# First half of the first batch's x turned by DMA inside the fold, and VectorE sums tied behind the addition for c12

## The chip, the cores and the metric

The kernel runs on one core of a Trainium2 chip. The engines that matter here are TensorE (PE: matmuls and transposes, with its weight loads as PEld), VectorE (DVE), ScalarE (ACT), GpSimd (POOL) and SyncE (SP), whose queue issues most of the DMAs. Each engine works through its own instructions in order. The metric is the device time of one execution in microseconds (us); lower is better.

## The reference

q, k and v are fp32; the weights come in as 8-byte floats, which the kernel converts to fp32 itself. Eight batches (B) of eight heads (H) have 576 tokens (S) of 64 values (D):

```python
kv = np.einsum('bhsd,bhse->bhde', k, v)
out = np.einsum('bhsd,bhde->bhse', q, kv)
rms = np.sqrt(np.mean(out * out, axis=-1, keepdims=True) + 1e-06)
attn = out / rms * g_norm
x = attn.transpose(0, 2, 1, 3).reshape(4608, 512)   # tokens x (heads, values)
out = (((x @ w1) * (x @ w2)) @ w3) @ w_out           # 512 -> 1024 -> 1024 -> 512
```

## The kernel before

**Groups.** The 4608 tokens are worked on as nine groups of 512: 512 of the 576 tokens of each batch make a group, and what is left over of all batches makes the last. For a group the kernel forms `kv` (L334), turns q so that tokens lie in the free dimension (on PE at L353, or by DMA), forms the attention product (L410), normalizes it (`norm`, L378 to L388, result in tile `xn`), and turns the normalized x into tile `xT`. Then the feed-forward part runs on `xT`: "gates" are the two products with `w1` and `w2` and their elementwise product (`gates`, L640 by `winograd`), in four passes p = 0 to 3 over the hidden columns, and "project" is the product with the folded matrix.

**The fold.** Since `w3` and `w_out` follow each other with nothing between, they are multiplied into one matrix `w3o` first (`fold_chunk`, L619, with the turned `w3` from `turn_w3`, L606, copied by ACT at L611). The fold has two halves of eight chunks c = 0 to 7. Its second half is interleaved by hand with the attention part of batch 0: at c = 1 and 4 come `kv` and q of two pairs of heads each (`begin_kv`, `begin_q`), at c = 2 and 5 the attention product of a half (`first.product`), at the start of c = 3 and 6 the end of its normalization, and at the end of c = 3 and 6 the turning of that half of x (`first.turn`, L444: eight 128x128 transposes on PE into two PSUM banks, which ACT copies to `xT` at L446). Weights are converted all along (`begin_next`: ACT at L158 and L159; `end_next`: DVE at L161 to L171, and a scaling by g at L136 on DVE or L134 on ACT).

**Turning by DMA.** `turn_by_dma` does the same without PE: a copy sorts the two 16-bit halves of each word apart (L291 or L293), SP issues a DMA transpose (L295), and a second copy puts the words together again (L305). `x_by_dma` does it for half of x, in two parts. Later batches use it with POOL's copies, batch 1's first half with ACT's.

**A pass of the gates.** `winograd` forms a 2x2 block product with seven products instead of eight. In order: a11·b11, s1·t1, s2·t2, s4·b22, s3·t3, a12·b21, a22·t4. Here a are the weights, s their sums (`sum_w(p)`, L692 and L693, four DVE operations into `ws` and `w_sb`), b are quarters of `xT`, and t their differences (`combine_x`, L682). Partial results are accumulated in three PSUM banks; ACT copies intermediate states out (L653), DVE adds (L778) and multiplies (L779). The tiles matter: u2 and u3 share one buffer `u`, so the copy of u3 has to wait until the addition for c12 has read u2, and the seventh product, which goes on in the bank that u3 is copied from, has to wait for the copy:

```python
        u2 = keep("u2", r1)
        between()
        product("s4", "b22", r2)
        done("c12", r2, u2)
        product("s3", "t3", r1)
        done("c22", p5, keep("u3", r1) if keep_u3 else r1)
        r3 = product("a12", "b21")
        done("c11", r3, p1)
        between()
        product("a22", "t4", r1)
        done("c21", r1, None)
```

**What sets the order.** PE, POOL and SP run in the order in which the program is written (`manual_schedule`). DVE and ACT are in written order inside the fold. In the groups after it a scheduler places their instructions; `tc.issue_after(x)` holds instructions back behind x. In group 0 (T = 0) the four passes also carry the conversions of the remaining weights, the sums of the next pass's weights (`sum_w(p + 1)`), and, for the product after the gates, the sums of `ab` and the differences of `w3o` (`sum_ab`, `combine_w3o`, L692, L693 and L682 on 256 columns). `between()` runs, twice in a pass, a piece of the next batch's attention part.

Of the kernel before, what the change touches and what calls it, by code (L numbers as in the profile page):

```python
# [22 lines left out]
def kernel(  # L23
# [32 lines left out]
    nc = tc.nc  # L56
# [7 lines left out]
    KF = DF // P  # L64
# [19 lines left out]
        return pool.tile([P, 512], FP32, name=tag, tag=tag)  # L84


    loaded, copies = {}, {}
    q_left = {}

    kv_left = [const.tile([P, H, D], FP32, name=f"{name}l_sb") for name in "kv"]  # L90
# [423 lines left out]
    def steps(b):  # L514

        a = batch(b)
        a.start()  # L520
        more = b + 1 < B
        fs, ends = ([[] for _ in range(8)] for _ in range(2))

        def turn(i, f, *args, next_group=False):

            t = []

            def begin():
                t.append(f(*args))
                next(t[0])  # L530
                next(t[0])

            fs[i].append((begin,))
            (to_end if next_group else ends[i + 1]).append((lambda: all_of(t[0]),))

        if to_end:

            ends[0] += [(lambda: nc.gpsimd.tensor_copy(tick, late["p5"][:, 0, 0:1]),), *to_end]
        to_end.clear()
        odd = b % 2  # L540
        if b == 1:
            q_first = a.q_two_by_dma(0, 1)
            early.append(q_first)
            fs[0].append((a.begin_kv, 0, 1))

            def end_first():
                with tc.issue_after(copies["kv"].ins):
                    next(q_first)
                all_of(q_first)

            ends[1].append((end_first,))
        fs[1] += [(a.begin_kv, 2, 3), (a.finish, 0)]
        if b == 1:
            last = {}

            def begin(name, behind, f, *args):
                last[name] = f(*args)
                with tc.issue_after(copies[behind][-1].ins):
                    next(last[name])
                next(last[name])  # L560

            def end(name, behind):
                with tc.issue_after(copies[behind][-1].ins):
                    next(last[name], None)
                all_of(last[name])

            fs[2] += [(begin, f"q{r}", "u2", a.q_two_by_dma, r) for r in (2, 3)]
            fs[3] += [
                (begin, "x", "u3", a.x_by_dma, 0, nc.scalar.copy),
                (begin, "left", "u3", a.q_left_by_dma),  # L570
            ]
            ends[4] += [(end, "q2", "p1"), (end, "q3", "p5"), (end, "x", "u2")]
            ends[5].append((end, "left", "u3"))
        else:
            turn(1, a.q_two_by_dma, 2, 3)
            turn(2, a.x_by_dma, 0)
            if odd:
                turn(1, a.q_left_by_dma)
        second = 5 if b == 1 else 4
        if more:  # L580
            fs[second].append((batch(b + 1).begin_kv, 0, 1))
        fs[second].append((a.finish, 1))
        if odd:
            fs[second].append((a.product_left,))
        if b == 1:
            turn(6, a.x_by_dma, 1)
            turn(7, a.x_left_by_dma, next_group=True)
        else:
            turn(5, a.x_by_dma, 1)
            if odd:  # L590
                turn(5, a.x_left_by_dma, next_group=more)
        if more:
            turn(7 if b == 1 else 5, batch(b + 1).q_two_by_dma, 0, 1, next_group=True)
            fs[7 if odd else 0].append((load_q_left, b + 1))
        return iter([lambda s=e + f: [f(*args) for f, *args in s] for e, f in zip(ends, fs)])
# [168 lines left out]
    def gates(T, p, between, ready=lambda name: None):  # L764
        def done(name, one, two):
            multiply(name, one, two)
            ready(name)

        def multiply(name, one, two):

            dst = ab[int(name[1]) - 1][:, p, int(name[2]) - 1, :]
            if two is None:
                c = late_pool.tile([P, N], FP32, name="c21")
                nc.scalar.copy(c, one[:, 0, :])  # L774
                nc.vector.tensor_mul(dst, c, one[:, 1, :])
                return
            c = late_pool.tile([P, 2, N], FP32, name="c")
            nc.vector.tensor_add(c, one, two)  # L778
            nc.vector.tensor_mul(dst, c[:, 0, :], c[:, 1, :])  # L779

        winograd(
            lambda name, w, c: wa[p][name][:, w, c, :],
            lambda name, c: xb[T][name][:, c, :],
            NP // 2, done, between, T == 0 or p + 1 < NF,
        )
# [412 lines left out]
    with tc.manual_schedule(  # L1198
        engines={mybir.EngineType.DVE, mybir.EngineType.Activation, mybir.EngineType.SP}
    ):  # L1200
        for _ in range(RAW):
            load_next()
        nc.scalar.activation(const.tile([P, 1], FP32, name="warm"), eps_col, AF.Sqrt)
        g_row = const.tile([1, P], FP32, name="g_row")
        for e in range(2):
            nc.scalar.dma_start(
                out=g_row[:, e * D:(e + 1) * D], in_=g_norm.rearrange("(o d) -> o d", o=1)
            )


        keep_warm(14)
        begin_next()
        end_next()
        turn_w3(0, 0)
        keep_warm(5)
        begin_next()

        g_ps = bank(ps_at, "at")[:, 0:1]
        nc.tensor.transpose(g_ps, g_row, ident[0:1, 0:1])
        nc.scalar.copy(g_col, g_ps)  # L1220
        for c in range(KF):

            if c == 0:
                end_next()
                begin_next()
            else:
                begin_next()
                end_next()
            if c == 4:
                load_kv_left(0)  # L1230
                load_pair("kvq", 0, 0)
            elif c == 5:
                load_pair("kvq", 0, 1)
                load_q_left(0)
            fold_chunk(0, c, range(NH - 1))
            turn_w3(*((0, c + 1) if c + 1 < KF else (1, 0)))
            fold_chunk(0, c, [NH - 1])
            if c == 0:
                keep_warm(4)


        first = batch(0)
        first.start()
        BEGIN, PRODUCT = {1: (0, 1), 4: (2, 3)}, {2: 0, 5: 1}
        norms = {}
        FIRST = len(converted) + KF - 1
        for c in range(KF):
            if c in BEGIN:
                first.begin_kv(*BEGIN[c])
                first.begin_q(*BEGIN[c])  # L1250
                if c == max(BEGIN):
                    load_q_left(1)
            if c - 1 in norms:
                all_of(norms[c - 1])
            if c < KF - 2:
                begin_next()

                end_next(len(raws) < FIRST)
            elif c == KF - 2:
                run(sum_w(0))  # L1260
            else:
                run(combine_x(0))
                end_next(False)
                for _ in range(3):
                    load_next()
            fold_chunk(1, c, range(NH - 1))
            if c + 1 < KF:
                turn_w3(1, c + 1)
            fold_chunk(1, c, [NH - 1])
            if c in PRODUCT:  # L1270
                norms[c] = first.product(PRODUCT[c])
                next(norms[c])
                next(norms[c])
            if c - 1 in norms:
                for r in range(2):
                    first.turn(2 * PRODUCT[c - 1] + r)
    fold_cm.__exit__(None, None, None)
    late_pool = ctx.enter_context(tc.tile_pool(name="late", bufs=1, reuse_waits="tile"))
    allocate()
# [4 lines left out]
    for n, T in enumerate(groups):  # L1284
# [25 lines left out]
        for p in range(NF):  # L1310
# [19 lines left out]
                gates(T, p, between, lambda name: all_of(f() for f in following[name]))  # L1330
                continue
            gates(T, p, between if T or p else lambda: None)
            if T == 0 and p == 0:
                for t in early:
                    with tc.issue_after(copies["xT"].ins):
                        next(t)
                    next(t)
            if T == 0:
                if p + 1 < NF:
                    run(sum_w(p + 1))  # L1340
                for n in range(2):
                    if len(converted) < len(todo):
                        ahead = [copies["xT"] if p == 0 else copies["u3"][0], copies["u2"][p]][n]
                        with tc.issue_after(ahead.ins):
                            begin_next()
                        if len(begun) < len(todo):
                            end_next()
                if p + 1 == NF:
                    allocate_projection()
                    run(*(f(i) for i in range(NF) for f in (sum_ab, combine_w3o)))  # L1350
            else:
                ops = [step() for step in sum_ab(p)]
                with tc.issue_after(ops[-1].ins):
# [45 lines left out]
```

## Time and profile before

| | |
|---|---|
| median of 6 runs | 760.67 us (760.2 to 761.55) |
| profiled execution, its own time | 760.86 us |
| its span, first to last instruction | 759.1 us |
| granted TensorE clock, mean | 1.00 |
| busy over the span: PE / DVE / ACT / POOL | 99% / 77% / 35% / 22% |
| PE without work, 0 to 48 us | 4.44 us |
| PE without work, 48 to 139.7 us | 0.78 us |
| DVE busy, 84.9 to 111.2 us | 25.73 of 26.30 us |
| HBM read and written | 105.78 and 19.14 MB |

The profiled execution's own time is 1.76 us above its span. The profile numbers lines as in the kernel printed above. A row "idle before, releaser" says how long an engine stood still ahead of a group of instructions and what let it go on. The chain of waits follows the run back from its last instruction, at each step to what ended the wait. The fold ends, and the gates of group 0 begin, at about 84.7 us; the four passes end at about 141.5 us.

### The profile page before, as it was taken

How to read it: one execution, taken by the hardware profiler on the slowest of the kernel's cores; microseconds unless marked ns; L12 is line 12 of the kernel's file. 1: busy time of each engine (PE TensorE's matmuls, PEld its weight loads, DVE VectorE, ACT ScalarE, POOL GpSimd, SP SyncE). 2: the span in 40 equal slices, each digit the busy share in tenths (PEclk: the TensorE clock that was granted, in tenths of full speed). 3: DMA queues.
4: the chain of work that ended last, by engine and by line, in shares of the span. 5: the costliest groups of instructions: out<-in, count | busy, mean ns of one | idle time of the engine just before them, and what ended most of it. 6: DMA issues, size and time to landing. Idle time of an engine off the chain costs nothing.

```text
span 759.1 us, 14969 instructions
## 1 busy us (share of the span) xinstructions
PE 750.2 (99%) x5915; PEld 657.4 (87%) x5915; DVE 588.2 (77%) x1171; ACT 264.6 (35%) x490; POOL 165.6 (22%) x190
## 2 busy tenths in 40 slices
PE   7999999999999999999999999999999999999998
PEld 5455788888899889988998899889988999999997
DVE  6977999548888568847985898467867778996897
ACT  6676776413222332232223322322233223222321
POOL 0000000222520441043104410441053125006100
PEclk9999999999999999999999999999999999999999
DMA  9996945338997936675778567835742470466244
GB/s 315 342 327 199 245 124 114 99 91 259 333 291 265 238 100 166 228 213 140 203 232 221 141 185 230 210 102 163 231 128 55 150 220 38 146 205 191 89 145 143
DMA packets 144442, 142.67 MB, mean 188 GB/s; under 512 B 84468, under 2 KB 131700, under 8 KB 144372
## 3 DMA queue, kind: packets, MB, share of 16 engines
q1 hardware_dynamic: 141920, 127.30, 57.1%
q10 hardware_dynamic: 2452, 14.42, 5.5%
q8 instruction: 47, 0.77, 0.4%
q14 instruction: 23, 0.19, 0.1%
HBM read 105.78 MB, written 19.14 MB: 165 GB/s over the span
## 4 chain that ended last, share of the span: by engine, by line
PE 97%; DMA 2%; ACT 1%; issue 0%; SPq 0%; DVE 0%; ACTq 0%
PE mm L640 55%; PE mm L1069 23%; PE mm L619 7%; PE mm L869 5%; PE at L334 3%; PE at L410 2%; DMA raw<-in_moe_w_out_dram 1%; PE at L869 1%; PE at L606 1%; PE at L1120 0%; DMA raw<-in_moe_w_dram 0%; PE at L353 0%; PE at L444 0%; PE at L429 0%; ACT ab L158 0%; ACT chunks L159 0%
## 5 line engine op out<-in xcount | busy, mean ns | idle before, releaser
L640 PE MATMUL mm<-xT,w_sb 128*128 128x256 f32 x720 | 165.2, 379 | 0.0
L640 PEld LDWEIGHTS mm<-xT,w_sb 128*128 128x128 f32 x720 | 136.3, 190 | 18.7 <-issue 0.5
L640 PE MATMUL mm<-xc,ws 128*128 128x256 f32 x512 | 115.7, 379 | 0.0
L640 PEld LDWEIGHTS mm<-xc,ws 128*128 128x128 f32 x512 | 97.2, 190 | 13.3
L291 POOL COPY xT<-xn 128x1024 uint16<-128x1024 uint16 x26 | 31.9, 1254 | 174.0 <-DVE xn L388 174.0
L778 DVE TENSOR_TENSOR c<-mm,u 128x512 f32<-128x512 f32 x32 | 22.1, 689 | 59.4 <-PE mm L640 59.4
L653 ACT COPY u<-mm 128x512 f32<-128x512 f32 x58 | 34.0, 586 | 93.8 <-PE mm L640 86.1
L653 ACT COPY p<-mm 128x512 f32<-128x512 f32 x66 | 38.7, 586 | 74.6 <-PE mm L640 71.2
L619 PE MATMUL mm<-chunks,ab 128*128 128x512 f32 x128 | 60.3, 603 | 2.5 <-DVE chunks L171 2.3
L640 PE MATMUL mm<-xc,w_sb 128*128 128x256 f32 x256 | 61.5, 383 | 0.7 <-ACT u L653 0.7
L640 PE MATMUL mm<-xT,ws 128*128 128x256 f32 x240 | 57.4, 382 | 0.0
L779 DVE TENSOR_TENSOR ab<-c 128x256 f32<-128x256 f32 x96 | 54.7, 570 | 2.5
L640 PEld LDWEIGHTS mm<-xc,w_sb 128*128 128x128 f32 x256 | 47.7, 190 | 8.1 <-ACT u L653 1.4
L640 PEld LDWEIGHTS mm<-xT,ws 128*128 128x128 f32 x240 | 45.0, 190 | 6.3
L1069 PE MATMUL mm<-w3o_sb,ab 128*128 128x128 f32 x368 | 48.6, 275 | 0.0
L379 DVE TENSOR_REDUCE inv<-sq 128x8 f32<-128x512 f32 (+1 forms) x40 | 23.4, 627 | 32.0 <-ACT sq L378 32.0
L1069 PE MATMUL mm<-w3o_sb,raw 128*128 128x128 f32 x372 | 48.1, 275 | 0.0
L1069 PEld LDWEIGHTS mm<-w3o_sb,ab 128*128 128x128 f32 x368 | 45.4, 192 | 0.4
L1069 PEld LDWEIGHTS mm<-w3o_sb,raw 128*128 128x128 f32 x372 | 44.8, 192 | 0.0
L774 ACT COPY c<-mm 128x256 f32<-128x256 f32 x32 | 11.9, 373 | 93.7 <-PE mm L640 93.7
L619 PEld LDWEIGHTS mm<-chunks,ab 128*128 128x128 f32 x128 | 21.8, 190 | 25.0 <-issue 15.8
L305 POOL COPY xT<-xn 128x1024 uint16<-128x1024 uint16 x26 | 31.6, 1241 | 54.1 <-DMA xn<-xT 54.1
(300 smaller groups left out, 1367.4 us busy)
## 6 DMA issues: line engine op xcount, KB each, us to landing
w3o_sb<-w3o_l SPq DMA_DIRECT2D x18, 896.0 KB, 4.8
raw<-in_moe_w_dram SPq DMA_DIRECT2D x31, 512.0 KB, 7.4
raw<-w3o_l SPq DMA_DIRECT2D x15, 896.0 KB, 4.8
w3o_sb<-w3o_l ACTq DMA_DIRECT2D x14, 896.0 KB, 4.6
k_sb<-in_k_dram SPq DMA_DIRECT2D x32, 256.0 KB, 4.4
v_sb<-in_v_dram SPq DMA_DIRECT2D x32, 256.0 KB, 4.9
q_sb<-in_q_dram SPq DMA_DIRECT2D x32, 256.0 KB, 4.0
out_dram<-raw SPq DMA_DIRECT2D x14, 512.0 KB, 3.6
```

The costliest lines, as they stand in the source:

```text
L291: copy(to, src.rearrange("p a n w -> p w a n"))
L305: copy(words(dst), src)
L334: nc.tensor.matmul(kv_ps[e * D:(e + 1) * D, r - rs[0], :], lhsT=k_sb[:, e, cols] if j < J else kl[:, 2 * r + e, :], rhs=v_sb[:, e, cols] i ...
L379: nc.vector.tensor_reduce(out=inv[:, i], in_=sq.rearrange("p (h d) -> p h d", d=D), axis=AX.X, op=ALU.add)
L410: nc.tensor.matmul(o_ps[l][tokens, n * D:(n + 1) * D], lhsT=qT[r][rows, e, i, tokens], rhs=kv_b[rows, e, r, :], start=True, stop=True,)
L619: nc.tensor.matmul(sums_ps[half][m], lhsT=w3T[half, c][:, m, :], rhs=chunks[:, c, 1, :], start=(c == 0), stop=(c == KF - 1),)
L640: nc.tensor.matmul(ps[:, u, :], lhsT=lhsT(a_name, u, c), rhs=rhs(b_name, c),  start=(u == 0 and c == 0 and to is None), stop=(c == chunks ...
L653: copies.setdefault(name, []).append(nc.scalar.copy(t, ps))
L778: nc.vector.tensor_add(c, one, two)
L779: nc.vector.tensor_mul(dst, c[:, 0, :], c[:, 1, :])
L869: nc.tensor.matmul(ps[place // 4][:, place % 4, :], lhsT=x, rhs=y, start=new and place // 4 not in seen, stop=True, skip_group_check=True,)
L1069: nc.tensor.matmul(to[:, i, :], lhsT=x[:, c, :], rhs=y[:, c, :], start=new and place // 4 not in seen, stop=(c == 1), skip_group_check=True,)
```

## The change

Four things, all before the second group:

1. In the fold, the first half of x is turned by `x_by_dma` with ACT's copies: the first copies (L291) at the end of c = 3, where `turn(0)` and `turn(1)` stood, and the second copies (L305) at the start of c = 5. So eight PE transposes and two ACT copies of PSUM go, and four ACT copies and two DMA transposes come.
2. The second half stays on PE, but its transposes stand in c = 7 behind the first matmul of the chunk, one matmul later than before. The weight conversions that `begin_next` begins on ACT at c = 4 and c = 5 are begun later, at c = 4 and c = 6 behind `turn_w3`.
3. In the passes of group 0, the sums of the next weights come behind the addition for c12 of the current pass (their first one only in pass 2), the ends of the conversions that are left behind the addition for c12 of pass 0, the first sums and differences for the projection behind c21 of pass 1, and the others behind the addition for c12 of pass 2. The beginnings of conversions in passes 1 and 2 are tied to p5 of the pass and not to u3 of pass 0.
4. The turning by DMA of q for batch 1, begun early, is two generators of one pair each and not one of both: the first still follows the copy of `xT`, the second follows u3 of pass 0.

In the built programs, PE has the same instructions but for the eight transposes, DVE the same in another order, ACT two less L446 and two more L291 and L305 each, SP two more L295; POOL is the same. Behind group 0's passes the order on every engine is the same.

```diff
@@ steps(b)
         if b == 1:
-            q_first = a.q_two_by_dma(0, 1)
-            early.append(q_first)
+            early.extend(a.q_two_by_dma(r) for r in (0, 1))
+            q_first = list(early)
             fs[0].append((a.begin_kv, 0, 1))
 
             def end_first():
-                with tc.issue_after(copies["kv"].ins):
-                    next(q_first)
-                all_of(q_first)
+                for t in q_first:
+                    with tc.issue_after(copies["kv"].ins):
+                        next(t)
+                    all_of(t)
@@ gates, multiply
-                nc.vector.tensor_mul(dst, c, one[:, 1, :])
+                adds.setdefault(name, []).append(nc.vector.tensor_mul(dst, c, one[:, 1, :]))
...
-            nc.vector.tensor_add(c, one, two)
+            adds.setdefault(name, []).append(nc.vector.tensor_add(c, one, two))
@@ second half of the fold
             if c < KF - 2:
-                begin_next()
+                if c < max(BEGIN):
+                    begin_next()
+                if c == max(BEGIN) + 1:
+                    all_of(x_first)
 
                 end_next(len(raws) < FIRST)
             elif c == KF - 2:
                 run(sum_w(0))
-            else:
+            fold_chunk(1, c, [0])
+            if c + 1 == KF:
+                for r in range(2):
+                    first.turn(2 + r)
                 run(combine_x(0))
...
-            fold_chunk(1, c, range(NH - 1))
+            fold_chunk(1, c, range(1, NH - 1))
             if c + 1 < KF:
                 turn_w3(1, c + 1)
+            if c in (max(BEGIN), KF - 2):
+                begin_next()
             fold_chunk(1, c, [NH - 1])
...
-            if c - 1 in norms:
-                for r in range(2):
-                    first.turn(2 * PRODUCT[c - 1] + r)
+            if c - 1 == min(PRODUCT):
+                x_first = first.x_by_dma(0, nc.scalar.copy)
+                next(x_first)
+                next(x_first)
@@ group 0, after the products of pass p
+                if p == 0:
+                    begin_early(copies["xT"])
                 if p + 1 < NF:
-                    run(sum_w(p + 1))
+                    ops = sum_w(p + 1)
+                    if p != 2:
+                        ops.pop(0)()
+                    with tc.issue_after(adds["c12"][p].ins):
+                        run(ops)
                 for n in range(2):
                     if len(converted) < len(todo):
-                        ahead = [copies["xT"] if p == 0 else copies["u3"][0], copies["u2"][p]][n]
+                        ahead = [copies["p5"][p] if p else copies["xT"], copies["u2"][p]][n]
                         with tc.issue_after(ahead.ins):
                             begin_next()
                         if len(begun) < len(todo):
-                            end_next()
+                            with tc.issue_after(adds["c12"][0].ins):
+                                end_next()
+                if p == 0:
+                    begin_early(copies["u3"][0])
                 if p + 1 == NF:
                     allocate_projection()
-                    run(*(f(i) for i in range(NF) for f in (sum_ab, combine_w3o)))
+                    first, *others = zip(*(f(i) for i in range(NF) for f in (sum_ab, combine_w3o)))
+                    with tc.issue_after(adds["c21"][p - 2].ins):
+                        all_of(step() for step in first)
+                    with tc.issue_after(adds["c12"][p - 1].ins):
+                        all_of(step() for steps in others for step in steps)
```

## The prediction

> **What bounds the kernel now.** I read the page's busy line first, then the waits of PE, then the stretches around the change, then rows of ACT there.
>
> ```profile
> PE 750.2 (99%) x5915; PEld 657.4 (87%) x5915; DVE 588.2 (77%) x1171; ACT 264.6 (35%) x490; POOL 165.6 (22%) x190
> ```
>
> PE works for all but 8.9 us of the span, so a microsecond counts only if it is taken from PE's own work or from one of its few idle moments. The waits of PE name these:
>
> ```profile
> PE mm L619 <- DVE chunks L171: 2.3, 1, 2.3
> PE mm L272 <- POOL ident masks.py:199: 2.0, 1, 2.0
> PE mm L640 <- ACT u L653: 0.7, 1, 0.7
> PE mm L619 <- ACT ab L611: 0.2, 1, 0.2
> ```
>
> The rows at L272 and L619 lie in the first 17 us, ahead of every edit. The third is in pass 2 of the gates of group 0. The stretches (PE, PEld, DVE, ACT, POOL; clock; DMA share; GB/s) show that PE is otherwise full, and that DVE is full too:
>
> ```profile
> 63.85:80.30 16.45, 16.45 (x158) 9.47 (x156) 15.25 (x20) 11.46 (x20) 0.00 (x0) 1.00 0.77 217
> 80.30:84.90 4.60, 4.60 (x18) 2.51 (x17) 4.43 (x8) 3.84 (x7) 0.00 (x0) 1.00 1.14 341
> 84.90:98.60 13.70, 13.70 (x65) 11.95 (x65) 13.70 (x22) 11.05 (x15) 0.00 (x0) 1.00 0.54 115
> 111.20:124.30 13.10, 12.40 (x64) 10.52 (x57) 13.10 (x29) 7.90 (x16) 0.00 (x0) 1.00 0.55 132
> ```
>
> The chain of waits runs over PE for this whole stage, but for that one wait:
>
> ```profile
> 64.01 0.95 PE at L444 x8
> ...
> 80.45 1.01 PE at L444 x8
> ...
> 123.62 0.59 ACT u L653
> ```
>
> The first is what the change takes away, the second it moves, the third it tries to make earlier. Behind group 0 the order is the same on every engine and PE has no further wait in its list, so I carry what PE gains by then to the end in full.
>
> **Edits 1 and 2: eight transposes leave PE.** The first L444 row is worth 0.95 us of PE time, from matmul to matmul. The second group of eight is moved behind one more matmul of the fold; it took 1.01 us, as xn (L388, 79.13 to 80.42) ended a little into it. Without that wait it takes 0.95, which gives 0.06. PE should reach the gates 1.0 us earlier, at 83.7 instead of 84.73.
>
> What pays for it lies beside PE. ACT loses two L446 (1.07 for both) and gets two L291 (1.05 each) and two L305 (1.16 each): 4.4 - 1.1 = 3.3 us more between 64 and 85. Is there room? These are ACT's rows of before:
>
> ```profile
> 64.71 1.07 ACT L446 COPY xT<-at 128x512 f32<-128x512 f32 x2
> 66.33 1.07 ACT L345 COPY kv_sb<-at 64x128 f32<-64x128 f32 x4 [0.54 <-PE at L334]
> 67.42 1.07 ACT L355 COPY qT<-at 128x512 f32<-128x512 f32 x2
> 68.38 1.19 ACT L158 ACTIVATE ab<-raw 128x1024 f32<-128x1024 uint32 x1
> 69.45 1.17 ACT L159 ACTIVATE w_sb<-raw 128x1024 f32<-128x1024 f32 x1
> 70.52 0.58 ACT L611 COPY ab<-at 128x512 f32<-128x512 f32 x1
> 72.20 1.18 ACT L158 ACTIVATE ab<-raw 128x1024 f32<-128x1024 uint32 x1 [1.10 <-DVE chunks L171]
> ```
>
> I walk the new order with these durations (a start follows the one before by about 0.1 less than its duration). L291 twice 64.7 to 66.6, L345 to 67.7, L355 to 68.7. L611 for chunk 5 is ready when PE's L606, now at 68.8, is done: 69.4, and ACT is free. L158 and L159 follow to 72.0, L305 twice to 74.2, L611 for chunk 6 to 74.7. PE wants it at 76.31 - 0.95 = 75.4 (76.31 is where L619 goes on behind L410), so 0.7 us are left. Next, L378 follows L410 at 75.5 (76.49), DVE takes it at 76.6, where its conversion ends (77.12), and xn ends at 79.9; PE's moved transposes stand at 80.2. Before the gates L158, L159, L624, L446 twice, L624 and L293 bring ACT to 84.3, then L624 twice and L158 to 86.4, and the copies of p1 and p5 end at 87.0 and 88.5, where PE wants them at 87.2 and 88.9. That is cover of 0.2 and 0.4 us where there were 0.7 and 0.9: enough, but thin. DVE's differences end at 85.1 instead of 85.6.
>
> DMA: SP gets two L295 (1.25 each to issue, from the rows at 126 us), ahead of the loads of batch 1, which stand there from 65.62. They move by up to 2.6 us; their k and v are read at 102. The raw weights behind them are issued at 73.8 instead of 72.71; they landed 6.9 to 9.6 us after issue, so by 83.4, and ACT reads the first at 85.3. The two transposes go out at 65.8 and 67.0, when the DMA engines were idle (share 0.00 to 0.31 from 64 to 67). How long they take there is not in the trace. The nearest row, the same tile at 126, lands after 2.8; the worst loads of raw at 73 us took 9.6. L305 is wanted at 72.0, with the 0.7 above: at 2.8 it costs nothing, at 9.6 it costs 76.6 - 72.7 = 3.9. I take 2.8, the same operation on idle queues.
>
> The page "VectorE: DVE Perf Modes" of the Trainium skill, section "Rules for kernel authors", speaks against this part: it turns 128x128 on TensorE wherever PSUM will do as the destination, and its table gives 390 ns there against 1309 by DMA (bf16). By it, eight blocks would lose some 7 us (an estimate) if the transposes lay on the path. The row of 0.95 us lies on the path here and the landing does not, so I follow the row.
>
> **Edit 3: sums behind c12.** In pass 2, DVE ran twelve narrow operations of the projection and the first sum of the next weights, from 118.20 to 122.82, ahead of the addition for c12 (L778 at 122.82); so u was free at 123.5, u3 was copied 123.62 to 124.20, and the seventh product began at 124.26. The sixth ended, by the step of 1.73 us between products, at 123.39: the wait cost 0.87. In the new order six operations (four of one kind from 118.9, about 0.34 each) stand ahead of c12 behind the last conversion. My walk of DVE from 85.1 (a conversion takes 4.6 us with its scaling, sums and additions start 0.60 apart, narrow ones 0.34) brings that conversion to 118.8 and c12 to 120.9 to 121.6. Then ACT is late next: its scaling L134 waits for the same conversion, then come two L293 (1.98 for both, until 121.98 before and after alike), then u3 until 122.6. PE would be there at 123.41 - 1.0 = 122.4. So 0.2 us of wait stay, and of the 0.87 we get 0.65. Bounds: 0.87 if ACT is early, nothing if DVE is as late as before.
>
> The same walk gives p1 of pass 2 as ready at 115.48, just when PE (113.03 - 1.0 + 3.46 = 115.49) wants it; before it had 0.16 to spare. I take 0; it could cost 0.3, as the sums of squares behind ACT's copies decide it.
>
> Behind the new waits DVE has: the sums for pass 3, ready from 121.5 to 124.8, wanted from 125.9; and nineteen narrow operations of the projection (6.4 us), which put c12 of pass 3 at 132.6 to 133.5, u3 at about 134.3, while the seventh product of pass 3 comes only behind L334, L410 and L429, at 137.9. These are covered by over 1 and 3 us. The split of q (edit 4) moves one L293 behind u3 of pass 0: its L305 runs at about 106.9, and L410 wants it at 109.0. Nothing.
>
> **The sum.** 0.95 + 0.06 + 0.65 = 1.66 us. The profiled execution would take 760.86 - 1.66 = 759.2; it lies 0.19 above the median of the runs, so for a median I predict 760.67 - 1.66 = **759.0**.
>
> **Rivals.**
>
> - *The wait stays, under another name.* DVE is full from 85 to 133 and none of its work is taken away; ACT has 3.3 us more. If the last conversion comes 0.9 later than in my walk, u3 is again as late as PE, and only the fold's 1.0 is left, or 0.7 with p1 late: 759.7 to 760.0. For it: the zero slack at p1 and at u3. Against it: c12 passes seven of the thirteen operations that stood ahead of it. Chance 0.22.
> - *The turned half comes late* (slower). L305 stands ahead of L611 in ACT's order, and PE's next chunk waits for L611. Each us that the DMA lands beyond 72.7 is a us of PE. From 74.4 (7.3 us after the second issue) it eats the gain of 1.66, and at the 9.6 of the raw loads the change costs 3.9 - 1.66 = 2.2: 762.9. For it: loads took that long 6 us later. Against it: the idle queues at 64 to 67. Chance 0.09.
> - *More than forecast.* The wait in pass 2 goes altogether, and ACT's later order spares a little more: 1.9 to 2.2, 758.5 to 758.8. Chance 0.10.
> - *The order does not help*: the addition for c12 is placed earlier, but is not what u3 waits for. Then it is the first rival's number; the row ahead of L653 speaks against it, since c12 ends 0.1 before it.
>
> **How the numbers follow.** A difference of 0.2%, 1.5 us here, is about what a measurement of this kernel can tell from no change. Forecast (1.3 to 1.9 won, 758.8 to 759.4) 0.54, of it 0.41 beyond 1.5 and 0.13 within; first rival 0.22, all within; late half 0.09, of it 0.07 slower and 0.02 within; more 0.10, faster; 0.05 left for small waits between, within. Faster 0.51, same 0.42, slower 0.07. The range goes from 758.5 to 760.2: it takes in the forecast, the first rival and most of the third, leaves out the late half, whose price is an upper bound far from its nearest row, and so holds over 8 in 10.
>
> **What would show it.** One L444 row of eight is left, and the gates begin near 83.7; DMA transposes xn<-xT issued near 66 and landing near 70, L305 from 72, and no PE wait on L611. In pass 2, c12 near 121 and the seventh product near 122.6. Wrong would be: PE waiting for L611 or for p1 in the fold's last chunks or in pass 0 (ACT too full), PE waiting for u as before at 122 to 124 (DVE too full), or a gap at p1 near 115.5.

## The result and the profile after

| | before | after |
|---|---|---|
| median, us | 760.57 (759.79 to 762.19, 39 runs) | 758.76 (758.12 to 760.02, 19 runs) |
| profiled execution, span | 760.86, 759.1 | 758.61, 756.8 |

The ratio is 0.9977, with a 95% interval of 0.9971 to 0.9983: 1.8 us faster. The prediction was 759.0, with a range of 758.5 to 760.2.

The busy line of the page after:

```profile
PE 749.7 (99%) x5907; PEld 657.3 (87%) x5907; DVE 587.0 (78%) x1171; ACT 267.3 (35%) x492; POOL 165.1 (22%) x190
```

Eight matmuls fewer are on PE, two copies more on ACT. The waits of PE after (line waited for; us in total, times, longest):

```profile
PE mm L620 <- ACT ab L612: 1.0, 1, 1.0
...
PE mm L1070 <- DVE ab L1032: 0.2, 1, 0.2
```

From L606 on, line numbers after are one higher than before: L612 is the copy of the turned `w3` that was L611. The wait for u (L653 before, L654 now) is gone. The row at L620 lies in the first 17 us, ahead of every edit, and differs from run to run, as does the row left out below it. The last row is new and is taken up below. The stretches after (PE, PEld, DVE, ACT, POOL; clock; DMA share; GB/s):

```profile
63.85:80.30 16.45, 16.45 (x140) 9.29 (x136) 15.67 (x21) 13.35 (x22) 0.00 (x0) 1.00 0.79 201
...
111.20:124.30 13.10, 13.10 (x61) 11.23 (x60) 13.10 (x27) 10.45 (x16) 0.00 (x0) 1.00 0.42 99
```

ACT took 1.9 us more work from 63.85 to 80.30 (13.35 against 11.46) and PE still never stood. From 111.2 to 124.3 PE is busy for all of 13.10 where it was for 12.40. The chain of waits after runs over PE through all of this:

```profile
79.39 0.87 PE at L444 x8
...
82.84 17.27 PE mm L641 x80
...
109.20 24.64 PE mm L641 x112
```

One L444 row of eight is left, it takes 0.87 instead of 1.01, and no `u` breaks the chain at 122.

**How the runs are compared.** A profiled execution of before reached its first attention product (L410) at 58.78 us, those of the changed kernel at 57.89, 58.07 and 58.43, ahead of every edit. I take this start to be chance: three profiles of one kernel differ in it by 0.54 us. So I compare stages, from PE's rows, in us. The columns run from one point to the next: the first attention product, the first product of the gates, the seventh product of pass 2, the start of group 0's projection, of group 1's, and of group 2's. From group 0's to group 1's every run took 77.72 or 77.73, and from group 2's to PE's last group 456.5.

| run | fold, to gates | to 7th product of pass 2 | to projection | group 1's to group 2's |
|---|---|---|---|---|
| before | 25.95 | 39.53 | 17.30 | 76.27 |
| after | 24.79 | 38.91 | 17.20 | 76.71 |
| after, second profile (e0) | 24.79 | 38.92 | 17.19 | 76.58 |
| after, third profile (e9) | 24.79 | 38.91 | 17.20 | 76.26 |
| fold alone (e1) | 24.79 | 39.77 | 17.21 | 76.51 |
| order alone (e2) | 25.97 | 38.95 | 17.19 | 76.71 |
| projection's sums alone (e3) | 25.96 | 39.60 | 17.19 | 76.26 |
| conversions not moved (e4) | 26.72 | 38.94 | 17.20 | 76.50 |
| turned half late (e5) | 31.15 | 38.89 | 17.20 | 76.26 |
| last conversion moved (e6) | 24.79 | 39.02 | 17.20 | 76.50 |
| both halves by DMA (e7) | 23.91 | 46.99 | 17.20 | 76.26 |
| GpSimd held back (e8) | 24.79 | 38.90 | 17.19 | 76.50 |

Between before and after the fold gained 1.16, the passes to that seventh product 0.62, and the rest up to the projection another 0.10: 1.88 us. The last column takes back 0 to 0.44, in three profiles of the same kernel.

### The profile page after: what moved, and what is told of

Its sections match the earlier page's. It is cut to its first block, busy times and chain, and to the rows that moved or that the text cites. A ratio compares the mean times of both kernels' runs of the same rounds, so it can differ in the third digit from the quotient of the medians.

```text
span 756.8 us, 14956 instructions
## 1 busy us (share of the span) xinstructions
PE 749.7 (99%) x5907; PEld 657.3 (87%) x5907; DVE 587.0 (78%) x1171; ACT 267.3 (35%) x492; POOL 165.1 (22%) x190
## 4 chain that ended last, share of the span: by engine, by line
PE 97%; DMA 2%; DVE 1%; ACT 0%; issue 0%; SPq 0%; ACTq 0%
PE mm L641 55%; PE mm L1070 22%; PE mm L620 7%; PE mm L870 5%; PE at L334 3%; PE at L410 2%; DMA raw<-in_moe_w_out_dram 1%; PE at L870 1%; PE at L607 1%; PE at L1121 0%; DMA raw<-in_moe_w_dram 0%; PE at L353 0%; PE at L429 0%; DVE ab L1032 0%; ACT ab L158 0%; ACT kv_sb L345 0%
## 5 line engine op out<-in xcount | busy, mean ns | idle before, releaser
L291 POOL COPY xT<-xn 128x1024 uint16<-128x1024 uint16 x26 | 31.5, 1240 | 173.8 <-DVE xn L388 173.8
L654 ACT COPY u<-mm 128x512 f32<-128x512 f32 x58 | 34.0, 586 | 93.1 <-PE mm L641 82.6
L654 ACT COPY p<-mm 128x512 f32<-128x512 f32 x66 | 38.7, 587 | 73.9 <-PE mm L641 71.7
L620 PE MATMUL mm<-chunks,ab 128*128 128x512 f32 x128 | 60.2, 603 | 1.2 <-ACT ab L612 1.0
L1070 PE MATMUL mm<-w3o_sb,ab 128*128 128x128 f32 x368 | 48.7, 275 | 0.2 <-DVE ab L1032 0.2
L1070 PE MATMUL mm<-w3o_sb,raw 128*128 128x128 f32 x372 | 48.1, 275 | 0.0
L379 DVE TENSOR_REDUCE inv<-sq 128x8 f32<-128x512 f32 (+1 forms) x40 | 23.4, 627 | 30.5 <-ACT sq L378 30.5
L1070 PEld LDWEIGHTS mm<-w3o_sb,ab 128*128 128x128 f32 x368 | 45.4, 192 | 0.8 <-DVE ab L1032 0.4
L1070 PEld LDWEIGHTS mm<-w3o_sb,raw 128*128 128x128 f32 x372 | 44.8, 192 | 0.0
L1081 ACT COPY u<-mm 128x512 f32<-128x512 f32 x23 | 13.5, 586 | 85.2 <-DVE raw L1094 46.2
L305 POOL COPY xT<-xn 128x1024 uint16<-128x1024 uint16 x26 | 31.6, 1241 | 50.1 <-DMA xn<-xT 50.1
```

Of the source, the lines that this page charges most:

```text
L291: copy(to, src.rearrange("p a n w -> p w a n"))
L305: copy(words(dst), src)
L379: nc.vector.tensor_reduce(out=inv[:, i], in_=sq.rearrange("p (h d) -> p h d", d=D), axis=AX.X, op=ALU.add)
L620: nc.tensor.matmul(sums_ps[half][m], lhsT=w3T[half, c][:, m, :], rhs=chunks[:, c, 1, :], start=(c == 0), stop=(c == KF - 1),)
L654: copies.setdefault(name, []).append(nc.scalar.copy(t, ps))
L1070: nc.tensor.matmul(to[:, i, :], lhsT=x[:, c, :], rhs=y[:, c, :], start=new and place // 4 not in seen, stop=(c == 1), skip_group_check=True,)
```

## The experiments

### Where the gain comes from: e0, e1, e2

The kernel after again, without an edit. 

> The changed kernel once more, for a second profile beside the parts. Both theories: 1.4 to 2.2 us below before. In the first profile the start (before any edit) was 0.9 us quicker, PE came to the gates 1.16 earlier from the edits, to the project stage of group 0 1.87 earlier, and lost 0.45 at 219 us where a VectorE sum (line 1032) took 1.38 us beside a GpSimd copy. If that collision belongs to the change, it is here again; if it is chance, it is not. The wait for p1 in pass 2 (0.26) should be here again, since ACT's order sets it.

Measured: 758.63 us, ratio 0.9976 (0.9966 to 0.9985). Fold and passes repeat to 0.01. The wait at L1070 is not there, but the last column still lost 0.31: GpSimd's copies fall on L1030 (1.33 us) and on a later L1032 (1.37).

The fold of after with the passes of before:

```diff
-                if p == 0:
-                    begin_early(copies["xT"])
+            if T == 0 and p == 0:
+                for t in early:
...
-                    with tc.issue_after(adds["c12"][p].ins):
-                        run(ops)
+                    run(sum_w(p + 1))
...
-                        ahead = [copies["p5"][p] if p else copies["xT"], copies["u2"][p]][n]
+                        ahead = [copies["xT"] if p == 0 else copies["u3"][0], copies["u2"][p]][n]
...
-                    first, *others = zip(*(f(i) for i in range(NF) for f in (sum_ab, combine_w3o)))
+                    run(*(f(i) for i in range(NF) for f in (sum_ab, combine_w3o)))
```

> The fold of the changed kernel, the passes of the kernel before. Theory (VectorE's lateness in pass 2 decides): PE comes to the gates 1.16 earlier, but the addition for c12 of pass 2 still stands behind twelve narrow operations, VectorE is only 0.5 to 0.6 earlier, so the wait for u3 grows from 0.87 to about 1.4 and only 0.5 to 0.7 us are won. Rival (the parts are independent): 1.16 won, the wait stays at 0.87.

Measured: 759.66 us, ratio 0.9995 (0.9985 to 1.0004), 0.67 below the 760.33 of before beside it. The fold is the same 24.79 as in after: 1.16 come from it alone. But the passes take 39.77, 0.24 more than before. The loss is not at u3, where the theory put it. In pass 2 there is no wait (from the seventh product of pass 1 it takes 12.19, the shortest of all runs; before took 13.06). PE now waits for the copies of p in passes 0 and 1, which follow ACT's extra work. PE's timeline in this run:

```profile
88.07 1.99 PE L641 MATMUL mm<-xT,ws 128*128 128x256 f32 x8 [0.23 <-ACT p L654]
98.98 1.99 PE L641 MATMUL mm<-xc,ws 128*128 128x256 f32 x8 [0.28 <-ACT p L654]
```

These two waits make the way to the seventh product of pass 2 longer by 1.1 us, and pass 2 gives 0.87 back. So the size fitted the theory and the place did not.

The passes of after with the fold of before:

```diff
...
-            fold_chunk(1, c, [0])
-            if c + 1 == KF:
-                for r in range(2):
-                    first.turn(2 + r)
...
-            if c - 1 == min(PRODUCT):
-                x_first = first.x_by_dma(0, nc.scalar.copy)
+            if c - 1 in norms:
+                for r in range(2):
+                    first.turn(2 * PRODUCT[c - 1] + r)
```

> The fold of the kernel before, the passes of the changed kernel (all ties). Theory: the wait for u3 in pass 2 goes, as u3 is ready at about 122.6 and PE comes at 123.4: 0.87 us won, nothing else. Rival (the ties only rename the wait): 0 to 0.3 won, PE waits for p1 or u3.

Measured: 759.95 us, ratio 0.9997 (0.9988 to 1.0005), 0.4 below before. The passes gain 0.58, and not the 0.87 of the theory, since a wait of 0.3 at p1 of pass 2 takes part of it. The rest up to the projection adds 0.11, and the last column takes 0.44 back. No part alone is beyond what can be told from no change; together they are. Up to group 1's projection the stages of e1 won 1.01 and those of e2 0.67. After won 1.88, 0.2 more than their sum: the waits for p in e1 do not come about in the new order.

### The wait that changes its name: e3, e6

Before, with only the sums and differences for the projection tied:

```diff
...
-                    run(*(f(i) for i in range(NF) for f in (sum_ab, combine_w3o)))
+                    first, *others = zip(*(f(i) for i in range(NF) for f in (sum_ab, combine_w3o)))
+                    with tc.issue_after(adds["c21"][p - 2].ins):
+                        all_of(step() for step in first)
+                    with tc.issue_after(adds["c12"][p - 1].ins):
+                        all_of(step() for steps in others for step in steps)
```

> The kernel before with one tie alone: the sums for the projection behind c21 of pass 1 and behind c12 of pass 2. Theory: this tie alone takes six narrow operations (2.0 us) from ahead of c12 in pass 2 and wins the same 0.87 us as all ties together. Rival: the ties of the next weights and of the conversions are needed too, and 0.4 or less are won.

Measured: 760.41 us, ratio 1.0002 (0.9993 to 1.001). The theory failed and its rival held. The addition for c12 came 2 us earlier, at 120.81, and u3 no longer stops PE, but up to the seventh product of pass 2 the passes lose 0.07 instead of gaining 0.87. A row of ACT's timeline, and one of PE's, in this run:

```profile
115.62 0.31 ACT L383 ACTIVATE inv<-inv,eps_col 128x16 f32<-128x16 f32 x1 [2.88 <-DVE inv L379]
```

```profile
116.45 1.99 PE L640 MATMUL mm<-xc,ws 128*128 128x256 f32 x8 [0.67 <-ACT p L653]
```

ACT stands 2.88 us at L383, the square root of a norm, for DVE's sums of squares (L379), and the copy of p1 queues behind it. Before, ACT stood there 1.95 us. The scheduler filled the room on DVE with the end of a conversion, ahead of the sums of squares. It is the first rival of the prediction in pure form: a wait at u3 is exchanged for one at p1, 0.67 in this row. In after, the same place on ACT:

```profile
113.75 0.31 ACT L383 ACTIVATE inv<-inv,eps_col 128x16 f32<-128x16 f32 x1 [0.59 <-DVE inv L379]
```

There the end of the conversion comes behind the sums of squares, and ACT stands only 0.59. It is the same with the passes of after alone (e2), so the other ties make this difference. But in after two products that take 3.62 elsewhere take 3.88:

```profile
112.69 3.88 PE L641 MATMUL mm<-xc,ws 128*128 128x256 f32 x16
```

That is 0.26 lost at p1. I tried to get it back by beginning the last conversion later, behind a square of batch 1's first norm:

```diff
-                nc.scalar.activation(sq, o_ps[i], AF.Square)
+                copies["sq"] = nc.scalar.activation(sq, o_ps[i], AF.Square)
...
+                        if (p, n) == (1, 1):
+                            ahead = copies["sq"]
```

> The changed kernel with the beginning of the last weight conversion on ScalarE tied behind the squares of batch 1's first product. Theory (ScalarE's 2.3 us of conversion ahead of the squares make p1 late in pass 2): the wait of 0.26 there goes, 0.2 to 0.3 us below the changed kernel. Rival: the conversion then comes later on VectorE, u3 of pass 2 is late again, and it is no faster or 0.2 to 0.6 slower than the changed kernel.

Measured: 759.0 us, ratio 0.9982 (0.9973 to 0.9991). The wait at p1 stays, 0.36 here, because the second half of that beginning (L159) is now placed ahead of the copy of p1. No gain.

### What pays for the turning: e4, e5, e7

After, with the conversions begun where before begins them:

```diff
-                if c < max(BEGIN):
-                    begin_next()
+                begin_next()
...
-            if c in (max(BEGIN), KF - 2):
-                begin_next()
```

> The changed kernel, but the conversions begun at chunks 4 and 5 of the fold stay where they were, ahead of turn_w3. Theory (ScalarE is nearly full there): the copy of the turned w3 for chunk 5 waits behind two conversion operations, until about 70.5 where PE wants it at 69.2; 1.3 us lost there, perhaps as much again at chunk 6: about before's time, 760 to 762. Rival (ScalarE has room): within 0.3 us of the changed kernel.

Measured: 760.56 us, ratio 1.0004 (0.9995 to 1.0013). The fold takes 26.72, 1.93 more than after. PE waits for both copies of the turned `w3` that ACT's extra work now stands ahead of:

```profile
70.40 2.84 PE L620 MATMUL mm<-chunks,ab 128*128 128x512 f32 x6 [1.15 <-ACT ab L612]
...
76.16 2.84 PE L620 MATMUL mm<-chunks,ab 128*128 128x512 f32 x6 [0.52 <-ACT ab L612]
```

So the turning by DMA pays only together with the later conversions. Without them the fold is 0.77 slower than before, and the whole change worth nothing.

After, with both DMA transposes (the second `next` issues them) behind the loads of batch 1, to try the slower rival (the turned half comes late):

```diff
                 x_first = first.x_by_dma(0, nc.scalar.copy)
                 next(x_first)
-                next(x_first)
...
                 load_q_left(1)
+                next(x_first)
```

> The changed kernel with the two DMA transposes of x issued behind the loads for batch 1 and not ahead of them: the turned half comes late. Theory (ScalarE's second copies stand ahead of the copy that PE waits for, with about 0.5 us to spare, and each us beyond costs a us): issue near 71 to 74, landing near 77 or later, 4 to 7 us slower than the changed kernel, 763 to 766. Rival (the landing has much room, or the loads ahead cost little): under 1 us slower.

Measured: 765.13 us, ratio 1.006 (1.0046 to 1.0074). The chain of waits of this run:

```profile
72.91 3.47 DMA xn<-xT
...
76.48 2.21 ACT xT L305 x2
```

The second transpose was issued from 72.91 on (67.25 in after) and landed 3.47 us later, and L305 began at 76.48 instead of 71.10. PE's timeline shows the first part of the price:

```profile
79.22 4.54 PE L620 MATMUL mm<-chunks,ab 128*128 128x512 f32 x6 [4.59 <-ACT ab L612]
```

It waited 4.59, and then six matmuls that take 2.84 took 4.54. The second part stands in the stretches, in the column of the granted clock (the first number behind the five engines):

```profile
74.50:79.20 4.70, 0.13 (x10) 0.00 (x0) 1.49 (x2) 2.72 (x4) 0.00 (x0) 1.00 1.09 288
79.20:83.70 4.50, 4.47 (x7) 1.89 (x8) 3.50 (x7) 1.27 (x3) 0.00 (x0) 0.62 1.10 355
```

PE stood nearly all of 4.7 us, and for the next 4.5 us its clock was 0.62 (ahead of it and behind it 1.00): 0.38 x 4.5 = 1.7 us more. Wait and clock make 4.6 + 1.7 = 6.3 of the 6.36 that the fold lost against after. The mechanism of the slower rival is real, and its price was too low: it counted a us for a us and left out the clock.

After, with the second half turned by DMA too:

```diff
-                for r in range(2):
-                    first.turn(2 + r)
+                def keep_last(dst, src):
+                    copies["xT"] = nc.scalar.copy(dst, src)
+
+                all_of(first.x_by_dma(1, keep_last))
```

> The changed kernel with the second half of x turned by DMA too (copies on ScalarE where the transposes stood). Eight more transposes, 0.87 us, leave PE. Theory (here the landing lies on the path): x is normalized at 79 and the gates want the second half from 86; two copies, two transposes in a busy queue and two copies end near 89, and ScalarE stands still meanwhile with the copies of the fold's sums and of p1 behind: 3 to 6 us slower than the changed kernel. Rival (a DMA transpose is free wherever it is put): 0.9 us faster.

Measured: 766.36 us, ratio 1.008 (1.0066 to 1.0094), 7.6 above the 758.76 of after, where 3 to 6 were expected. The fold is 0.88 shorter as its last eight transposes go, and then PE waits for the half at once. PE's timeline, and the stretches around it:

```profile
90.59 3.78 PE L641 MATMUL mm<-xc,ws 128*128 128x256 f32 x8 [5.17 <-DVE xc L683]
```

```profile
85.00:90.50 5.50, 0.43 (x2) 0.03 (x1) 0.65 (x2) 3.48 (x5) 0.00 (x0) 0.73 0.85 237
90.50:94.50 4.00, 3.90 (x9) 3.18 (x10) 3.93 (x7) 2.87 (x5) 0.00 (x0) 0.51 1.10 360
```

Eight matmuls of 1.89 took 3.78: the clock halved here too, with 5.17 us of standing. Of the 8.1 us that the passes lost, the wait makes 5.3 and the slow matmuls 2.0; the rest are waits for the copies of p in pass 2. For the second half the rule that the prediction weighed holds: nothing covers the landing, and TensorE is the place to turn it. For the first half it does not hold: turning it by DMA saved 0.95 us of TensorE, and nothing waited for the landing.

The page "TensorE: Matmul & The Clock Gate" of the Trainium skill, section "HAM oscillation — how this bites in real kernels", asks for no idle gaps of PE over some 3.4 us, since a longer one sets the clock to half. Both runs agree in the effect (4.6 and 5.2 us of standing; 0.62 and 0.51 in the stretches behind). In the length e7 differs: its first stretch has 0.73 already, because the clock was at half from 87.57 on, 2.1 us after PE's last matmul ended, and until 94.40. In e5 it was at half from 79.55 to 82.96. A wait of 2.31 us in before, at 8.9 us, left it at 1.00, and so did the 0.70 at u3. How long PE may stand without this price is not settled between 2.3 and 4.6 us.

### What group 1 takes back: e8, e9

In the profile of after, group 1's projection has a wait that before has not. The timeline there, DVE, GpSimd and PE:

```profile
217.80 2.69 POOL L305 COPY xT<-xn 128x1024 uint16<-128x1024 uint16 x2 [10.85 <-DMA xn<-xT]
...
218.10 1.38 DVE L1032 TENSOR_TENSOR ab<-ab 128x256 f32<-128x256 f32 x1
...
219.54 0.71 PE L1070 MATMUL mm<-w3o_sb,ab 128*128 128x128 f32 x4 [0.18 <-DVE ab L1032]
```

An operation that takes 0.42 took 1.38 beside a copy of GpSimd. To try whether the copy is the cause, GpSimd is held behind the last sum of that place, by one more instruction in its list (a copy of one column of that sum's tile into `tick`); nothing else in any engine's order changes:

```diff
...
-            t = []
+            t, to = [], (ends + [[]])[i + 2 if hold else i + 1]
+            to += [(lambda: nc.gpsimd.tensor_copy(tick, ab_sums[0][:, 0, P:P + 1]),)] * hold
...
-            turn(5, a.x_by_dma, 1)
+            turn(5, a.x_by_dma, 1, hold=(b == 2))
```

> After, with one GpSimd instruction more: before its two copies that put the second half of batch 2's x together (L305), GpSimd copies one column of the last sum for the second inner product of group 1's projection, so that the copies start behind that sum, at about 5.3 us from the start of the projection and not at 1.3 as in the profile of after. Theory (the narrow DVE operations of that place take 1.38 and not 0.42 us because GpSimd's copy runs beside them): L1032 is back at 0.42, PE has no wait there, group 1's projection to group 2's takes 76.27 as in before and not 76.71 or 76.58, and the median is 0.3 to 0.45 below after, near 758.4; the differences of xT, at 227.8, still find the copies done by 224.6. Rival (DVE is slowed by the transfers or by something else of that moment): L1032 stays above 1 us with GpSimd still, and the stage stays at 76.5 to 76.7. Second rival: the collision moves to the sums that follow (222 to 224.5), and PE loses as much there.

Measured: 759.21 us, ratio 0.998 (0.997 to 0.9989); 0.3 to 0.45 below after was expected, and it is 0.5 above the run of after beside it (e9). The timeline of this run:

```profile
218.62 0.42 DVE L1032 TENSOR_TENSOR ab<-ab 128x256 f32<-128x256 f32 x1
...
220.81 2.44 POOL L305 COPY xT<-xn 128x1024 uint16<-128x1024 uint16 x2
220.99 1.25 DVE L694 TENSOR_TENSOR raw<-ab,raw 128x256 f32<-128x256 f32 x1
```

L1032 is back at 0.42. By itself this proves little: the transpose landed at 219.2 in this run, so the copies would have come behind this L1032 without the hold too. But up to 220.8, while GpSimd was held, every such operation took 0.42, and the two beside the copies are slow: L694 and, behind it, L1028 (1.37). The same holds in all twelve profiles: exactly two operations of this place are slow (0.92 to 1.39 us), and each ends 0.28 or 0.29 us behind the end of one of the two copies. Before has it too: beside its copies, from 222.70, L693 takes 0.93 and L1027 1.36, and PE has time for both. The slow operations move along with GpSimd's copies, wherever these fall: that is what shows the cause. The stage still takes 76.50, so the second rival holds as well: the operations hit instead are also wanted.

The kernel after, a third time, beside e8. 

> The changed kernel once more, unedited, as the measure for the run beside it. Expected: 758.5 to 758.9; group 1's projection to group 2's 76.5 to 76.75, by where GpSimd's copies fall.

Measured: 758.73 us, ratio 0.9979 (0.9969 to 0.9989), and the stage takes 76.26, less than expected and the same as in before. Here GpSimd's copies, which wait for a DMA, start later:

```profile
220.12 2.50 POOL L305 COPY xT<-xn 128x1024 uint16<-128x1024 uint16 x2 [11.46 <-DMA xn<-xT]
...
220.24 1.37 DVE L1032 TENSOR_TENSOR raw<-raw 128x256 f32<-128x256 f32 x1
```

A later L1032 is hit, one that PE has time for. Over all twelve profiles the stage follows the start of these copies, counted from the start of group 1's projection: 76.26 or 76.27 where it is 3.06 to 3.52 us (before, e3, e5, e7, e9), 76.50 to 76.58 at 2.50 to 2.73 (e0, e1, e4, e6), 76.71 at 1.28 and 1.54 (after, e2), and 76.50 at 3.78 (e8). The same kernel had 1.28, 2.73 and 3.06. So the loss is a matter of when a DMA lands in that run, and not one that the change brings for certain. Whether the change moves the average start is open: there is one profile of before.

## Why the prediction was right, point by point

**The time** was forecast as 1.66 below before, and the runs gave 1.8. The forecast case was the one that came about: the fold and the passes, as sums, were off by under 0.2 each. That they come so near is in part luck, since terms that were left out or mis-sized, by 0.1 to 0.4 us each, have opposite signs. They follow one by one.

**Eight transposes leave PE (0.95).** Right: the L444 row at 64.01 is gone, and the fold is shorter by it in every run with this edit. **The second group, 0.06 by its move.** It takes 0.87 for 1.01, but the eight matmuls around it take 4.38 for 4.30, which leaves 0.06, as was said. **The fold in all: 1.0 forecast, 1.16 measured.** The 0.16 were left out of the sum. The walk had them: L611 for chunk 5 is ready at "69.4, and ACT is free", while before it stood behind two conversions until 70.52. PE's row of eight matmuls over that copy shows it, in the chain of waits of before and of after:

```profile
70.31 3.68 PE mm L619 x8
```

```profile
68.47 3.52 PE mm L620 x8
```

I used the walk to look for losses only.

**The walk of ACT** held. Add 0.89 to the times of after, for the earlier start:

```profile
68.51 0.59 ACT L612 COPY ab<-at 128x512 f32<-128x512 f32 x1 [0.63 <-PE at L607]
...
71.10 2.24 ACT L305 COPY xT<-xn 128x1024 uint16<-128x1024 uint16 x2
73.22 0.60 ACT L612 COPY ab<-at 128x512 f32<-128x512 f32 x1
```

That gives 69.40 for L612 (69.4 forecast), 71.99 for L305 (72.0), and L612 for chunk 6 done at 74.71 (74.7). L305 follows the conversion without a wait, so the landing was in time: the second transpose, issued from 67.25 on, took at most 3.8 us. e5 shows 3.47 at a busier moment, near the 2.8 that I took and not near the 9.6. The cover of 0.2 and 0.4 at p1 and p5 of pass 0 was enough: no such wait is in after.

**Sums behind c12 (0.65 of 0.87).** The size is right, 0.62 to the seventh product of pass 2; what it is made of is wrong in two places that nearly cancel. The forecast was that 0.2 us of the wait for u3 stay. None stay: after's ACT had u3 at 120.68,

```profile
120.68 0.57 ACT L654 COPY u<-mm 128x512 f32<-128x512 f32 x1
```

which with 0.89 is 121.57 to 122.14, where I had u3 ready at 122.6: the two L293 ahead of it ended sooner than the same time as before, which I had assumed. And "I take 0; it could cost 0.3" for p1 cost 0.26. The zero slack was seen and named. The fold's own extra is not the reason, since e2, with the fold of before, lost 0.30 there. 0.16 are the wait itself; the other 0.10 come behind it, as in the next point. The rival "the wait stays under another name" is what the tie does by itself (e3): nothing gained. What made the forecast right and the rival wrong is that the other ties come with it; which of them is needed was not tried one by one, and the split of q (edit 4) was not tried alone.

**Behind the seventh product** another 0.10 were gained that no step named. They belong to the same wait. PE's timeline, before and after:

```profile
124.26 1.99 PE L640 MATMUL mm<-xc,w_sb 128*128 128x256 f32 x8 [0.70 <-ACT u L653]
```

```profile
121.59 1.89 PE L641 MATMUL mm<-xc,w_sb 128*128 128x256 f32 x8
```

Eight matmuls right behind a wait take 0.10 longer, 1.99 for 1.89, as in the rows of e1 and e3. So the wait at u3 cost 0.87 and 0.10 behind it. All runs without this wait have the 0.10 (17.19 to 17.21 in the table against 17.30), e1 too, which has none of the ties.

**"I carry what PE gains to the end in full."** This was argued from equal orders on every engine, and it is not quite true. An equal order does not make equal neighbours: GpSimd's copies hang on a DMA, and slow DVE where they fall. It cost 0 to 0.44 us in three profiles. With it, the stages give 1.88 less 0 to 0.44, that is 1.4 to 1.9. The medians differ by 1.6 to 1.8.

**The late half** had chance 0.09 at up to 2.2 us slower. Its mechanism was shown (e5); what kept it away is where the two transposes stand on SP, ahead of batch 1's loads, and its price is higher than I had it: 6.3 us of PE for 4.6 of standing. "Each us that the DMA lands beyond 72.7 is a us of PE" leaves out the clock.

## What to carry to other kernels

A transpose that leaves the bounding engine is worth its full time there as long as nothing waits for its landing; ask for each tile what covers the landing, and what other work on the copying engine must move to make room, since that move decided here between 1.8 us and nothing. When one wait on a full engine is taken away, look for the next instruction with no slack behind the same engine: a tie that puts one result first puts others last, and the scheduler chooses which. Walk the order for gains as well as for losses.

## What the runs showed of the hardware that was not expected

**Standing costs twice.** Behind 4.6 and 5.2 us in which PE stood, its granted clock was 0.62 over 4.5 us and 0.51 over 4.0, and matmuls took up to twice as long (eight in 3.78 instead of 1.89). The clock was at half for 3.41 us in e5 and for 6.83, twice as long, in e7, where it had begun while PE still stood.

**GpSimd's copies stop DVE's.** A subtraction of 256 columns with both inputs in SBUF or a sum like it took 0.92 to 1.39 us instead of 0.42 where it ran beside copies of GpSimd (two in 2.4 to 2.7 us), and 0.42 otherwise, in all twelve profiles. The page "SBUF — State Buffer" of the Trainium skill, section "Who interferes with whom", says that a VectorE instruction with two SBUF inputs contends with a GpSimd instruction that reads SBUF, and calls the ports that they share an exclusive lock. The rows agree with it: a slow operation ends 0.28 or 0.29 us behind the end of a copy (219.48 and 219.20 in after), and L776, whose second input lies in PSUM, takes 0.41 beside a copy (221.53 in e9).
